# Position bias by four float32 column products instead of masks and three-piece products, in a fused attention, expert and cosine layer

## The chip, the cores and the metric

The kernel runs on one core of one Trainium2 chip. The metric is the device time of one execution in microseconds; lower is better. The engines named below are TensorE (PE, its weight loads PEld), VectorE (DVE), ScalarE (ACT), GpSimd (POOL) and the queue that issues transfers (SP).

## The reference, cut to what matters

```python
psi_rel = np.log1p(np.abs(pos[:, None] - pos[None, :]))        # S x S, S = 576
psi_i   = np.log1p(np.maximum(pos[:, None], 1.0))
x = (psi_rel / psi_i)[..., None]
h = np.maximum(x @ w1 + b1, 0.0)                               # 32 hidden values per (i, j)
bias = h @ w2                                                  # 8 heads
attn = softmax(q @ k.T / 8 + bias);  x = attn @ v              # 2 batches, 8 heads, 64 wide
out += p[:, e] * (relu(x @ w1[e]) @ w2[e])                     # 4 experts, 512 -> 1024 -> 512
h = x @ w_in;  y = (h * cos(h)) @ w_out                        # 512 -> 2048 -> 512
```

There are 1152 tokens (2 x 576).

## The kernel before, in words

Nothing in the file is written in the order in which it runs. `build` records steps (`G.step`), each with an engine, a planned duration, what it reads and writes, and a priority, and `Graph.order` then runs a list scheduler over them: whenever an engine is free it takes the ready step with the lowest priority number, with planned delays between engines. Steps with `alts` may go to a second engine after a planned wait. The instructions are issued in that order, so a changed planned duration moves instructions on every engine.

The work comes in three stretches. In the first, `bias_step` runs 36 times. Step s covers 16 query positions; 128 partitions hold 4 positions x 32 hidden values, four such groups t = 0..3 make a step. The width W of a step is 576, 512, 384 or 448 keys, the rest is mirrored from other steps. A mask per group says where the hidden value is positive: groups 0 and 1 by DVE (L508), groups 2 and 3 by ACT as a sign (L510), both written as bf16. PE multiplies the masks by two weight sets (w1*w2 and b1*w2), each cut into three bf16 pieces (L532): four column tiles of 32 columns, one for each t, which write 32 partitions of PSUM each. Two DVE operations (L540, L547) combine the two products with the table `tab2` and the row factor `nrec`. The result is stored to DRAM (`biasD`, mirrored parts to `biasR`) and later loaded again by each attention unit. Besides, `first_set` works out attention of the first 64 queries, in float32, of all heads and both batches, and `fill` runs the experts for these 128 tokens in float32, one half of an expert (512 hidden columns) at a time; NFILL of the 8 halves are done so.

In the second stretch `second_set` works out attention of the other 512 queries (float32 operands in fp32r form, each as a high and a low part, three products); its last product is at L745. Fills and expert jobs stand between its pieces on PE. In the third stretch come the experts for 2 x 512 tokens, and the cosine layer. A half of an expert is either plain (12 products of 512 columns for each 128 hidden columns and 512 tokens, L798) or blocked: `block_products` (L938) gets both 512-token blocks of the first layer with 7 products in place of 8, from sums that `block_tokens` and `block_weights` prepare. The second layer is L807 for all. NHALF halves are plain, NFILL - NHALF are blocked, the rest take in the first 128 tokens as well.

Of the kernel before, what the change touches and what calls it, by code (L numbers as in the profile page):

```python
# [33 lines left out]

class Buf:
# [18 lines left out]
class Graph:  # L54
    LAG = {"PE": 215.0, "ACT": 160.0, "DVE": 165.0, "POOL": 160.0, "DMA": 100.0}
    TO_PE = {"ACT": 250.0, "DVE": 245.0, "POOL": 175.0, "DMA": 207.0}
    SWITCH, STAY = {"columns": 93.0, "rows": 196.0, "": 196.0}, 0
# [48 lines left out]

    def order(self):
        steps = self.steps
# [32 lines left out]
        while len(out) < len(steps):  # L141
# [16 lines left out]
            for e in engs:  # L158
# [47 lines left out]
                if e == "PE" and s.mode != mode:  # L206
                    s.dur, mode = s.dur + max(0.0, self.SWITCH[s.mode] - (now - eng_free[e])), s.mode
# [6 lines left out]
                tp = s.end + s.lat + self.TO_PE.get(e, 0.0)  # L214
                heapq.heappush(events, t)
                for k in s.succ:
                    same = k.eng == s.eng == "PE"
                    k.rdy = max(k.rdy, s.end if same else tp if k.eng == "PE" else t)
                    k.nd -= 1
                    if k.nd == 0:  # L220
                        offer(k)
# [29 lines left out]
def t_col(n):  # L251

    return n / 2.4 + 3.0
# [20 lines left out]
NFILL = 7  # L274

NHALF = 2
# [3 lines left out]
FKEEP = 2  # L280
# [3 lines left out]
NWAIT = 8  # L284
SIGNED = ((36, (2, 3)),)
# [3 lines left out]
NH, NW, NB, NF, NEARLY = 8, 12, 5, 16, 14  # L289

P_GEN, P_ADD, P_SPA, P_SPD, P_E32, P_REL, P_SUB, P_NRM, P_EV, P_REV, P_TWO = 200.0, 2500.0, 150.0, 1500.0, 300.0, 300.0, 2000.0, 3000.0, 1000.0, 200.0, 0.0

O_GEN, O_SGN, O_STT, O_ADD, O_SPL, O_EVC, O_NRM = 80, 0, -150, 0, 150, -10, 0

BAHEAD, HAHEAD, FAHEAD, BACK, BACK0, G_SET, G_FILL, G_MAIN = 5, 3, 3, 4, 2, 33, 6, 1
# [30 lines left out]
def shape_constants():  # L326
# [10 lines left out]
    c = np.concatenate([tab, tab2, nrec, np.eye(128, dtype=np.float32)], axis=1)  # L337
# [3 lines left out]
NCONST = 1148 + 1136 + 36  # L341
# [3 lines left out]
def build(ctx: ExitStack, tc: tile.TileContext, consts, q, v, qd, kp, vp, w12, probs, mw1, mw2, win, wout, out):  # L345
# [10 lines left out]
    biasR = {i0: T(dr, [1032, w], F32, f"biasR{i0}") for i0, w in RW.items()}  # L356
    planes = {nm: T(dr, sh, F32, nm + "hl") for nm, sh in (
# [7 lines left out]
    w32 = T(sb, [128, 128], F32, "w32")  # L365
    wrm = w32[:, 64:128]
    wph = w32[:, 0:96].bitcast(BF16).rearrange("p (k n) -> p k n", k=3)
    hcol = w32[:, 96:98].bitcast(BF16)
    wpc = T(sb, [128, 3, 64], BF16, "wpc")
    cneg = T(sb, [128, 144], F32, "cneg")  # L370
    cpos = T(sb, [128, 144], F32, "cpos")
# [4 lines left out]
    kc = T(sm, [128, 3 + len(SIGNED)], F32, "kc")  # L376
    ca = kc[:, 3:3 + len(SIGNED)]
# [23 lines left out]
    G.add_class("B", [T(pb_, [128, 2304], BF16, f"bs{i}") for i in range(NB)])  # L401
    cst = T(pb_, [128, NCONST], F32, "cst")
    tab = cst[:, 0:1148]
    tab2 = cst[:, 1148:2284]
    nrec = cst[:, 2284:2320]
# [16 lines left out]
    def dma(nbytes, fn, **kw):  # L422
        return G.step("DMA", t_dma(nbytes), fn, lat=LAT, **kw)
# [6 lines left out]
    dma(128 * 640 * 4, lambda: nc.sync.dma_start(out=cst[:, 508:1148], in_=consts[:, 508:1148]), wr=[(cb, "r1")])  # L430
    dma(128 * 1172 * 4, lambda: nc.sync.dma_start(out=cst[:, 1148:2320], in_=consts[:, 1148:2320]), wr=[(cb, "t2")])
    dma(128 * 508 * 4, lambda: nc.sync.dma_start(out=cst[:, 0:508], in_=consts[:, 0:508]), wr=[(cb, "r0")])
    dma(18432, lambda: nc.sync.dma_start(out=prob, in_=probs.rearrange("p (t e) -> p t e", e=NE)), wr=[fix("prob")])
    dma(128 * 128 * 4, lambda: nc.sync.dma_start(out=ident, in_=consts[:, 2320:2448]), wr=[fix("ident")])
# [9 lines left out]
    for kk in range(2):  # L444
        G.step("DVE", 130, lambda kk=kk: nc.vector.tensor_scalar(
            out=w32[:, 32 * kk:32 * kk + 32], in0=wpad, scalar1=prm[:, kk:kk + 1], scalar2=(1.0, 8.0)[kk], op0=ALU.mult, op1=ALU.mult),
            rd=[fix("prm")], wr=[(fix("w32"), kk)], port=True)
    for kk in range(3):
        src = w32[:, 0:64] if kk == 0 else wrm
        G.step("DVE", 130, lambda kk=kk, src=src: nc.vector.tensor_copy(wpc[:, kk, :], src), rd=[fix("w32")], wr=[fix("w32"), fix("wpc")], port=True)  # L450
        if kk < 2:
            G.step("DVE", 130, lambda kk=kk, src=src: nc.vector.tensor_tensor(out=wrm, in0=src, in1=wpc[:, kk, :], op=ALU.subtract),
                   rd=[fix("w32")], wr=[fix("w32")], port=True)
    G.step("DVE", 180, lambda: nc.vector.tensor_scalar(out=wph, in0=wpc, scalar1=0.5, scalar2=None, op0=ALU.mult),
           rd=[fix("wpc")], wr=[fix("w32"), fix("wph")], port=True)
    G.step("DVE", 120, lambda: (nc.vector.memset(hcol[:, 0:2], 0.5), nc.vector.memset(hcol[:, 2:4], 0.0)), rd=[fix("wph")], wr=[fix("w32"), fix("hcol")])
    cp = Buf("P1")

    def half_sums():
        for j, (_, ts) in enumerate(SIGNED):  # L460
            for i in range(3):
# [29 lines left out]

    def bias_step(s, back, p2, gates=()):

        u_, mk = Buf("E"), Buf("B")
        sj, ts = signed(s)
        ka, kb = key_range(s)
        W = kb - ka
# [870 lines left out]
```

## Time and profile before

| | |
|---|---|
| median of 3 runs | 794.1 us (793.37 to 860.72) |
| the profiled execution, its own time | 796.37 us |
| its span in the trace | 794.6 us |
| PE busy | 778.1 us (98%), 5134 matmul records |
| DVE busy | 667.7 us (84%) |
| ACT busy | 446.6 us (56%) |
| POOL busy | 162.7 us (20%) |
| granted TensorE clock | 1.0 in all 40 slices of the span |

A matmul's record is longer than the time until the next one can start, so a busy share of 98% doesn't mean that PE has no time left to lose. Where a price of a matmul is needed, it is taken from long unbroken runs of one kind: their time divided by their count.

### The profile page before, as it was taken

How to read it: one execution, taken by the hardware profiler on the slowest of the kernel's cores; microseconds unless marked ns; L12 is line 12 of the kernel's file. 1: busy time of each engine (PE TensorE's matmuls, PEld its weight loads, DVE VectorE, ACT ScalarE, POOL GpSimd, SP SyncE). 2: the span in 40 equal slices, each digit the busy share in tenths (PEclk: the TensorE clock that was granted, in tenths of full speed). 3: DMA queues.
4: the chain of work that ended last, by engine and by line, in shares of the span. 5: the costliest groups of instructions: out<-in, count | busy, mean ns of one | idle time of the engine just before them, and what ended most of it. 6: DMA issues, size and time to landing. Idle time of an engine off the chain costs nothing.

```text
span 794.6 us, 14995 instructions
## 1 busy us (share of the span) xinstructions
PE 778.1 (98%) x5134; PEld 647.6 (81%) x5134; DVE 667.7 (84%) x1560; ACT 446.6 (56%) x942; POOL 162.7 (20%) x215
## 2 busy tenths in 40 slices
PE   7899999999999999999999999999999999999998
PEld 6476667887888888887888888888889889998997
DVE  8978978998999997766997979799789949959575
ACT  7677468888887533334462627263635637545352
POOL 0121077788755520234000000000000000000000
PEclk9999999999999999999999999999999999999999
DMA  6898999788865214645644346344473297547012
GB/s 194 288 289 249 297 285 307 225 280 265 267 193 186 80 54 136 206 150 185 226 146 154 124 159 201 111 139 168 145 244 108 85 339 250 174 136 262 27 40 80
DMA packets 98988, 148.08 MB, mean 186 GB/s; under 512 B 13280, under 2 KB 46688, under 8 KB 98912
## 3 DMA queue, kind: packets, MB, share of 16 engines
q1 hardware_dynamic: 98912, 147.13, 57.0%
q8 instruction: 40, 0.66, 0.4%
q14 instruction: 36, 0.29, 0.1%
HBM read 110.68 MB, written 36.41 MB: 185 GB/s over the span
## 4 chain that ended last, share of the span: by engine, by line
PE 73%; DVE 10%; DMA 8%; ACT 4%; issue 3%; SPq 1%; DVEq 0%; ACTq 0%
PE p1x L807 18%; PE p L807 12%; PE p1x L938 8%; PE p1x L798 7%; PE p L938 7%; PE p L798 4%; PE p L532 4%; PE p L745 3%; PE p L677 2%; PE p L725 2%; DMA fs<-in_mw 2%; PE p L1053 2%; DMA biasD<-es 1%; ACT es L650 1%; PE p L1061 1%
## 5 line engine op out<-in xcount | busy, mean ns | idle before, releaser
L807 PE MATMUL p1x<-wx,hs 128*128 128x512 f32 (+1 forms) x792 | 185.1, 389 | 0.5 <-DVE fs L1018 0.5
L807 PEld LDWEIGHTS p1x<-wx,hs 128*128 128x128 f32 x792 | 147.3, 188 | 31.9 <-DVE fs L1018 0.9
L807 PE MATMUL p<-wx,hs 128*128 128x512 f32 (+1 forms) x432 | 102.9, 389 | 0.2 <-DVE hs L1004 0.2
L807 PEld LDWEIGHTS p<-wx,hs 128*128 128x128 f32 x432 | 79.7, 188 | 16.6 <-DVE hs L1004 0.6
L798 PE MATMUL p1x<-xh,wx 128*128 128x512 f32 (+2 forms) x272 | 79.0, 361 | 1.3 <-DVE hs L1004 1.2
L660 POOL TENSOR_SCALAR es<-es,stats 128x576 f32<-128x576 f32 (+2 forms) x102 | 62.8, 632 | 44.6 <-DVE stats L654 17.3
L573 ACT ACTIVATE wx<-fs 128x512 fp32r<-128x512 f32 (+1 forms) x83 | 46.4, 581 | 32.3 <-DMA fs<-in_mw 20.6
L650 ACT ACTIVATE es<-es,stats 128x576 f32<-128x576 f32 x72 | 55.3, 770 | 10.6 <-DVE stats L647 4.2
L532 PE MATMUL p<-bs,wpc 128*32 128x288 bf16 (+3 forms) x576 | 51.1, 323 | 7.4 <-DVE es L547 3.6
L798 PEld LDWEIGHTS p1x<-xh,wx 128*128 128x128 f32 x272 | 50.0, 188 | 7.9 <-DVE hs L1004 2.5
L647 DVE CUSTOM_DVE_ANT_0 es<-p,es 128x576 f32<-128x576 f32 x72 | 53.0, 749 | 3.8 <-PE p L725 1.4
L574 DVE TENSOR_TENSOR wx<-fs,wx 128x512 fp32r<-128x512 f32 (+1 forms) x68 | 44.2, 674 | 9.7 <-ACT wx L573 9.7
L532 PEld LDWEIGHTS <-wpc 128*32 128x32 bf16 x576 | 30.8, 97 | 23.5 <-issue 14.2
L532 PE MATMUL p<-bs,w 128*32 128x288 bf16 (+3 forms) x576 | 49.9, 322 | 0.0
L510 ACT ACTIVATE bs<-cst,cpos 128x576 bf16<-128x576 f32 (+3 forms) x72 | 45.6, 694 | 7.2 <-PE p L532 4.7
L798 PE MATMUL p1x<-xl,wx 128*128 128x512 f32 (+2 forms) x136 | 48.9, 359 | 0.0
L938 PE MATMUL p1x<-xh,wx 128*128 128x512 f32 (+1 forms) x140 | 45.7, 368 | 0.0
L585 DVE TENSOR_TENSOR hs<-p,hs 128x512 fp32r<-128x512 f32 x61 | 41.3, 686 | 3.7 <-ACT hs L583 3.1
L573 ACT ACTIVATE fs<-fs 128x256 fp32r<-128x256 f32 x54 | 21.8, 413 | 39.7 <-DVE fs L1127 39.6
L677 PE MATMUL p<-ident,es 128*128 128x128 f32 x276 | 42.2, 280 | 0.4 <-ACT x L707 0.3
L798 PE MATMUL p<-xh,wx 128*128 128x384 f32 (+2 forms) x144 | 39.9, 341 | 0.0
L677 PEld LDWEIGHTS p<-ident,es 128*128 128x128 f32 x276 | 30.4, 140 | 10.8 <-issue 6.1
(232 smaller groups left out, 1751.2 us busy)
## 6 DMA issues: line engine op xcount, KB each, us to landing
fs<-in_mw SPq DMA_DIRECT2D x123, 256.0 KB, 4.4
wx<-winhl SPq DMA_DIRECT2D x32, 256.0 KB, 4.7
wx<-wouthl SPq DMA_DIRECT2D x32, 256.0 KB, 3.9
wouthl<-fs SPq DMA_DIRECT2D x29, 256.0 KB, 2.4
fs<-in_win SPq DMA_DIRECT2D x28, 256.0 KB, 4.2
es<-biasD SPq DMA_DIRECT2D x24, 288.0 KB, 3.9
fs<-in_wout SPq DMA_DIRECT2D x27, 256.0 KB, 3.5
winhl<-fs SPq DMA_DIRECT2D x25, 256.0 KB, 2.8
```

The source lines that it names most:

```text
L510: G.step("ACT", t_act(W, 1, 1), lambda w0=w0, u=u, t=t: nc.scalar.activation(out=mask(t), in_=tab[:, w0:w0 + W], func=AF.Sign, bias=cpos[: ...
L532: nc.tensor.matmul(out=pv(a)[32 * t:32 * t + 32], lhsT=w[:, i, 32 * kk:32 * kk + 32], rhs=mask(t, m * a, m), start=(i == 0), stop=(i == 2) ...
L573: act = ("ACT", t_act(n, 0, 1), lambda: nc.scalar.activation(out=hv(), in_=fv(), func=AF.Copy))
L574: low = lambda e: e.tensor_tensor(out=lv(), in0=fv(), in1=hv().bitcast(F32), op=ALU.subtract)
L585: G.step("DVE", t_dve(n), lambda: nc.vector.tensor_tensor(out=dst(AL), in0=src(), in1=dst(AH).bitcast(F32), op=ALU.subtract), rd=[ps_, (AH ...
L647: G.step("DVE", t_dve(S) + 10, lambda: nc.vector.tensor_tensor_reduce(out=f3(bt.tile[:, :S]), in0=sp.tile[:, :, 0:288], in1=f3(bt.tile[:, ...
L650: exp_all.append(G.step("ACT", t_act(S, 1, 1) + 104, lambda: nc.scalar.activation(out=e.tile[:, :S], in_=bt.tile[:, :S], func=AF.Exp, scal ...
L660: nrm = lambda g: g.tensor_scalar(out=dst(), in0=src(), scalar1=rs, scalar2=1.0, op0=ALU.mult, op1=ALU.mult)
L677: nc.tensor.transpose(tp.tile[:, 128 * kt:128 * kt + 128], e.tile[:, 128 * kt:128 * kt + 128], ident)
L798: nc.tensor.matmul(out=z.tile[:, 0:n], lhsT=w[dt][2][wi]()[:, 128 * ft:128 * ft + 128], rhs=x[:, dt, p0:p0 + n], start=(dt == 0 and i == 0 ...
L807: nc.tensor.matmul(out=y.tile[:, 0:m], lhsT=hx, rhs=w[ft][2][wi]()[:, c0:c0 + m], start=(ft == 0 and i == 0), stop=(ft == nf - 1 and i == 2))
L938: nc.tensor.matmul(out=z.tile[:, 0:n], lhsT=x()[:, 128 * t:128 * t + 128], rhs=y(), start=(start and d == 0 and i == 0), stop=(d == 1 and ...
```

## The change

The masks go. Each group's hidden value itself, relu(w1*psi_rel + b1*psi_i), is written in float32 (DVE by add and max, ACT by Relu; either may take it), PE multiplies it by the padded w2 in one float32 matmul per column tile, and one scaling by `nrec` (ACT, or DVE) evacuates the product. The weight pieces, the half sums and `tab2` fall away. Then: NFILL 7 to 8 and NHALF 2 to 1, so that seven halves of experts are blocked in place of five; `block_tokens` loads the whole float32 values, stored to DRAM beforehand (`x1D`, `x2D`), in place of adding up high and low parts (14 DVE operations for each of four blocks become 8); the planner's delays and durations are changed, and 17 seeded changes of priorities (`MOVES`) are made ahead of planning.

```diff
     def order(self):
+        for m in MOVES:
+            self.move(m)
...
-NFILL = 7
-NHALF = 2
+NFILL = 8
+NHALF = 1
...
-        u_, mk = Buf("E"), Buf("B")
+        u_, hid = Buf("E"), [Buf("B"), Buf("B")]
...
-                e.tensor_scalar(out=mask(t), in0=tab[:, w0:w0 + W], scalar1=cneg[:, u:u + 1], scalar2=None, op0=ALU.is_ge)
-                    out=mask(t), in_=tab[:, w0:w0 + W], func=AF.Sign, bias=cpos[:, u:u + 1]), rd=rdt + [fix("cpos")], wr=[(mk, t)], after=gate, off=O_SGN)
+            act = ("ACT", t_act(W, 1, 1), lambda w0=w0, u=u, t=t: nc.scalar.activation(
+                out=hv(t), in_=tab[:, w0:w0 + W], func=AF.Relu, bias=cpos[:, u:u + 1]))
+            dve = ("DVE", t_dve(W, 1, True), lambda w0=w0, u=u, t=t: nc.vector.tensor_scalar(
+                out=hv(t), in0=tab[:, w0:w0 + W], scalar1=cpos[:, u:u + 1], scalar2=0.0, op0=ALU.add, op1=ALU.max))
...
-            def mm(kk=kk, pv=pv):
-                for i in range(3):
-                    for a in range(npc):
-                        for t in range(4):
-                            w = wph if t in ts else wpc
-                            nc.tensor.matmul(out=pv(a)[32 * t:32 * t + 32], lhsT=w[:, i, 32 * kk:32 * kk + 32], rhs=mask(t, m * a, m),
-                                             start=(i == 0), stop=(i == 2), tile_position=(0, 32 * t))
+        def mm():
+            for a in range(npc):
+                for t in range(4):
+                    nc.tensor.matmul(out=pv(a)[32 * t:32 * t + 32], lhsT=wpad, rhs=hv(t, m * a, m), start=True, stop=True, tile_position=(0, 32 * t))
+        bias_mm[s, 0] = G.step("PE", 4 * npc * t_col(m), mm, rd=hid + [fix("prm")], wr=[pb], mode="columns")
...
-        G.step("DVE", t_dve(W, 1), lambda: nc.vector.scalar_tensor_tensor(
-            G.step("DVE", t_dve(n, 1), lambda pc=pc, uv=uv, n=n: nc.vector.scalar_tensor_tensor(
+        G.step("ACT", t_act(W, 1), lambda: nc.scalar.activation(out=uo(), in_=pi(), func=AF.Copy, scale=nrec[:, s:s + 1]),
+               rd=[pb, (cb, "r1")], wr=[(u_, 0)], off=O_STT,
+               alts=[("DVE", t_dve(W, 1), lambda: nc.vector.tensor_scalar(
...
+        x1_st[p, b] = dma(128 * Q1 * 4, lambda: nc.sync.dma_start(out=x1D[p, :, Q1 * b:Q1 * b + Q1], in_=x32.tile[:, :Q1]), rd=[x32])
...
+                dma(128 * n * 4, lambda: nc.sync.dma_start(out=b.tile[:, 0:n], in_=whole[dd, :, n * c:n * c + n]), wr=[b], after=stored(dd, c) + after)
```

On PE the first bias step reads as follows before; `bs` are the masks, `wpc` and `w_76` the bf16 pieces of the weights, `p_160` a bank pair in PSUM, and this pattern comes back for each of three pieces, for both halves of the width, and for both weight sets:

```order
L532 LDWEIGHTS wpc
L532 MATMUL p_160<-bs_147,wpc 32x288
L532 LDWEIGHTS wpc
L532 MATMUL p_160<-bs_147,wpc 32x288
L532 LDWEIGHTS w_76
L532 MATMUL p_160<-bs_147,w_76 32x288
L532 LDWEIGHTS w_76
L532 MATMUL p_160<-bs_147,w_76 32x288
```

In the same place of the changed kernel the first four rows are one whole step (two halves of the width, four tiles each) and the fifth begins the next; `bs` are now hidden values, `prm` holds the padded w2, and a row with x2 is two column tiles:

```order
L506 MATMUL p20_160<-bs0_146,prm_77 32x288 x2
L506 MATMUL p20_160<-bs4_150,prm_77 32x288 x2
L506 MATMUL p20_160<-bs0_146,prm_77 32x288 x2
L506 MATMUL p20_160<-bs4_150,prm_77 32x288 x2
L506 MATMUL p21_161<-bs1_147,prm_77 32x288 x2
```

A step of two halves has gone from 48 matmuls, piece after piece with the four tiles in turn, to 8 float32 ones, each tile complete before the next begins; the whole program has 1152 and 192.

On DVE, early in the program, masks (L508) stand before between the combinations of the two products (L540, L547) and the first softmax operations (L647, L654, L656):

```order
L508 TENSOR_SCALAR bs_148<-cst,cneg 128x512 x2
L540 SCALAR_TENSOR_TENSOR es_143<-p_153,kc,cst 128x512
L508 TENSOR_SCALAR bs_147<-cst,cneg 128x384
L647 ISA es_137,stats<-p_160,es_137 128x576
L647 ISA stats 128x1
L508 TENSOR_SCALAR bs_147<-cst,cneg 128x384
```

After the change the rows of that stretch are nearly all hidden values (L495), while on ACT (the second piece) hidden values (L493) and evacuations (L511) take turns:

```order
L495 TENSOR_SCALAR bs_146<-cst,cpos 128x512
L495 TENSOR_SCALAR bs_148<-cst,cpos 128x512
L495 TENSOR_SCALAR bs_146<-cst,cpos 128x512
L470 RECIPROCAL psum_p<-psum_p 128x9
L495 TENSOR_SCALAR bs_147<-cst,cpos 128x512
```

```order
L493 ACTIVATE bs0_146<-cst_152,cpos_78 128x576
L511 ACTIVATE es1_128<-p21_161,cst_152 128x576
L493 ACTIVATE bs1_147<-cst_152,cpos_78 128x576
L511 ACTIVATE es2_129<-p20_160,cst_152 128x576
L493 ACTIVATE bs2_148<-cst_152,cpos_78 128x512
```

In all, DVE has 90 hidden values and 13 evacuations where it had 72 masks and 80 combinations, and ACT has 54 and 23 where it had 72 signs. In the order after, 6 units of the first 64 queries have passed ACT before its last bias operation, 8 before.

On PE behind the last attention product (L745 before, L711 after; `ht` is its last operand) the order before goes on with the experts' second layer:

```order
L745 MATMUL p1x_3823<-ht_95,ks_120 128x256
L807 MATMUL p1x_3832<-wx_3041,hs_90 128x512
L807 MATMUL p1x_3832<-wx_3042,hs_90 128x512
L807 MATMUL p1x_3832<-wx_3041,hs_90 128x512
L807 MATMUL p1x_3832<-wx_3276,hs_94 128x512
```

and after the change with pieces of fills (L1022, L1014), among first-layer products (L765):

```order
L711 MATMUL p_156<-ht_94,ks_119 128x256
L1022 MATMUL p_153<-fs_99,fs_113 128x512
L1022 MATMUL p_153<-fs_105,fs_113 128x512
L1022 MATMUL p_153<-fs_103,fs_113 128x512
L765 MATMUL p_156<-xh,wx_2200 128x512
```

Parts of the last three fills (32 float32 matmuls at L1014, 12 at L1022) now stand behind the attention, where none stood before.

## Rows read from the trace of the kernel before

**Rows 1.** The page's first part: busy time and share of each engine.
```profile
PE 778.1 (98%) x5134; PEld 647.6 (81%) x5134; DVE 667.7 (84%) x1560; ACT 446.6 (56%) x942; POOL 162.7 (20%) x215
```

**Rows 2.** Busy time by stretch; the second line names the columns.
```profile
core 0: us, PE busy (x) PEld busy (x) DVE busy (x) ACT busy (x) POOL busy (x), PEclk, DMA share, GB/s
0.00:102.20 102.20, 93.51 (x1411) 66.32 (x1412) 89.52 (x216) 66.76 (x131) 12.93 (x25) 1.00 0.83 263
102.20:258.20 156.00, 153.34 (x1205) 125.30 (x1205) 140.69 (x412) 126.60 (x294) 111.88 (x153) 1.00 0.81 251
258.20:794.60 536.40, 531.25 (x2520) 455.95 (x2519) 437.51 (x934) 253.30 (x518) 37.91 (x38) 1.00 0.46 153
```

**Rows 3.** Lines L532 and L745: count, ns min/median/max, first and last start.
```profile
L532 PE MATMUL p<-bs,w x576: 286/326/441, 6.5 to 101.8; 128*32 128x288 bf16 x96, 128*32 128x448 bf16 x40, 128*32 128x512 bf16 x32, 128*32 128x384 bf16 x24
L745 PE MATMUL p1x<-ht,ks x1: 283/283/283, 257.9 to 257.9; 128*128 128x256 f32 x1
```

**Rows 4.** Bias products by shape: count, busy us, mean ns, idle before.
```profile
L532 PE MATMUL p<-bs,w 128*32 128x288 bf16 x288 | 20.1, 289 | 0.0
L532 PE MATMUL p<-bs,w 128*32 128x448 bf16 x120 | 12.4, 353 | 0.0
L532 PE MATMUL p<-bs,w 128*32 128x512 bf16 x96 | 11.6, 380 | 0.0
L532 PE MATMUL p<-bs,w 128*32 128x384 bf16 x72 | 6.9, 327 | 0.0
```

**Rows 5.** Bias matmuls and weight loads in order of time: start us, us.
```profile
71.53 0.37 PE L532 MATMUL p<-bs,wpc 128*32 128x448 bf16 x2
...
71.72 0.37 PE L532 MATMUL p<-bs,wpc 128*32 128x448 bf16 x2
...
83.30 0.10 PEld L532 LDWEIGHTS <-w 128*32 128x32 bf16 x2
...
83.42 0.29 PE L532 MATMUL p<-bs,wpc 128*32 128x288 bf16 x2
83.54 0.29 PE L532 MATMUL p<-bs,wpc 128*32 128x288 bf16 x2
```

**Rows 6.** Unbroken runs in the chain that ended last: start us, us, what.
```profile
1.05 5.06 PE p L439 x22
170.11 1.79 PE p L1053 x16
188.72 1.72 PE p L1061 x4
679.78 4.16 PE p1x L798 x24
717.75 5.44 PE p1x L807 x24
```

**Rows 7.** DVE groups of 0 to 102.2 us: busy us, mean ns, idle before.
```profile
L508 DVE TENSOR_SCALAR bs<-cst,cneg 128x576 bf16<-128x576 f32 (+3 forms) x72 | 31.7, 468 | 0.1
L547 DVE SCALAR_TENSOR_TENSOR es<-es,cst,p 128x288 f32<-128x288 f32 (+4 forms) x43 | 26.7, 630 | 0.8 <-PE p L532 0.7
L540 DVE SCALAR_TENSOR_TENSOR es<-p,kc,cst 128x576 f32<-128x576 f32 (+3 forms) x36 | 25.7, 725 | 3.7 <-PE p L532 2.4 <-DMA biasD<-es 1.1
```

**Rows 8.** ACT groups of 0 to 102.2 us, and one evacuation of later.
```profile
L510 ACT ACTIVATE bs<-cst,cpos 128x576 bf16<-128x576 f32 (+3 forms) x72 | 45.6, 694 | 7.2 <-PE p L532 4.7 <-DVE wpc L450 1.6 <-ACT bs L510 0.7
L650 ACT ACTIVATE es<-es,stats 128x576 f32<-128x576 f32 x8 | 6.2, 776 | 6.7 <-DMA biasD<-es 2.2 <-DVE stats L647 1.2 <-PE p L692 1.2
...
L589 ACT ACTIVATE es<-p 128x512 f32<-128x512 f32 (+1 forms) x9 | 4.6, 523 | 1.0 <-PE p L677 0.8
...
L583 ACT ACTIVATE hs<-p 128x512 fp32r<-128x512 f32 x61 | 35.6, 593 | 6.1 <-PE p L677 5.3
```

**Rows 9.** Whom PE waited for in 0 to 102.2 us: total, times, longest.
```profile
PE p L532 <- DVE es L547: 3.6, 3, 1.8
```

**Rows 10.** Line L473, a DVE operation that writes float32: ns min/median/max.
```profile
L473 DVE TENSOR_SCALAR cst<-cst,prm x2: 484/518/552, 4.1 to 6.8; 128x640 f32<-128x640 f32 x1, 128x508 f32<-128x508 f32 x1
```

More of the change, by code (lines that the diff above doesn't have):

```diff
@@ L105, in step, with move @@
         return s
+    def move(self, seed):
+        r = random.Random(seed)
+        lines = sorted({s.line for s in self.steps})
+        n = len(self.steps)
+        line, first, share = r.choice(lines), r.randrange(-n // 10, n), r.choice((0.01, 0.03, 0.1, 0.3, 1.0))
+        kind, by = r.random(), r.choice((-1, 1)) * r.choice((3, 10, 30, 80, 200, 500))
+        for s in self.steps[max(first, 0):max(first + int(n * share), 0)]:
+            if s.line != line:
+                continue
+            if s.lat and kind < 0.5:
+                s.lat = max(1500.0, s.lat + 5 * by)
+            elif len(s.alts) > 1 and kind < 0.5:
+                s.alts = s.alts[:1] + [(*a[:3], max(0.0, a[3] + 5 * by)) for a in s.alts[1:]]
+            else:
+                s.prio += by
     def order(self):
+        for m in MOVES:
+            self.move(m)
         steps = self.steps
@@ L422, in dma @@
     def dma(nbytes, fn, **kw):
[L423 removed]
+        return G.step("DMA", t_dma(nbytes), fn, lat=LAT if kw.get("wr") else LATS, **kw)
     def f3(t, n=2):
@@ L499, in bias_step @@
         m = W // npc
-        mask = lambda t, c0=0, n=W: mk.tile[:, 576 * t + c0:576 * t + c0 + n]
+        hv = lambda t, c0=0, n=W: hid[t // 2].tile[:, 576 * (t % 2) + c0:576 * (t % 2) + c0 + n]
         gate = list(gates) + ([bias_mm[s - back, 0]] if (s - back, 0) in bias_mm else [])
+        ts = next(x for end, x in ON_ACT if s < end)
         for t in range(4):
@@ L890, in block @@
-            two(lambda: xl[:, d, c1], t4v, lambda: xh[:, d, c1].bitcast(F32), ALU.subtract, [t4, (fix(t4n), (d, "h"))], [(fix(t4n), (d, "l"))], n,
-                after=done + last_l1)
+                return x
+            (b22, v22), (b12, v12), (b11, v11), (b21, v21) = load(d + 2, 1), load(d, 1), load(d, 0), load(d + 2, 0)
+            u = Buf("F")
+            uv = lambda: u.tile[:, 0:n]
+            x = two(uv, v22, v12, ALU.subtract, [b22, b12], [u], n)
+            keep_("T3", uv, u)
+            two(v12, v12, v11, ALU.subtract, [b12, b11], [b12], n, after=[x])
@@ new lines, in block @@
+            x = [x, keep_("T1", v12, b12)]
+            two(v22, v22, v12, ALU.subtract, [b22, b12], [b22], n, after=x)
+            keep_("T2", v22, b22)
+            two(v21, v21, v22, ALU.subtract, [b21, b22], [b21], n)
+            G.step("ACT", t_act(n, 0, 1), lambda: nc.scalar.activation(out=xh[:, d, c1], in_=v21(), func=AF.Copy),
+                   rd=[b21], wr=[(fix(t4n), (d, "h"))], after=last_l1)
+            two(lambda: xl[:, d, c1], v21, lambda: xh[:, d, c1].bitcast(F32), ALU.subtract, [b21, (fix(t4n), (d, "h"))], [(fix(t4n), (d, "l"))], n,
+                after=last_l1)
@@ L1258, in build @@
     run_ff(jobs, m2_ev1, m2_ev2, xr2)
-    tk2 = block_tokens(pcols, lambda d, x: range(3 * x + 3, 3 * x + 6), NP, [], ("x2h", "x2l"), "t4b")
+    tiles = lambda d, c: range(3 * c + 3, 3 * c + 6)
+    tk2 = block_tokens(pcols, tiles, NP, x2D, lambda d, c: [x2_st[t] for t in tiles(d, c)], [], ("x2h", "x2l"), "t4b")
     for c in range(NCONV, LATE):
```

200 lines of the change are left out of this document (64 added, 136 removed).

## The prediction

> **What bounds the kernel now.** I read the page's first part, then busy time by stretch, then in each stretch what its engines wait for. PE is busy 98% of the span and no other engine over 84% [rows 1]. But busy time of overlapping matmul records hides lost time, so I cut the span at two places that the change touches: the last bias product, whose matmul starts at 101.8 us, and the last attention product, which starts at 257.9 us [rows 3]; with the matmuls' own length the cuts are 102.2 and 258.2. The reader should see three different stretches [rows 2].
>
> In the last one (536.4 us) PE runs 2520 matmuls back to back. Runs of one kind give prices: 24 products of 512 columns take 5.44 us, 0.227 each, and 24 of 384 take 4.16, 0.173 each [rows 6]; 256 columns are 0.120 on the same line. The 2520 matmuls (1824 of 512, 588 of 384, 72 of 256, 36 transposes at the 0.11 of a float32 record of 128 columns) come to 528 us, so only 8 us are lost there, the end included. That stretch is PE's.
>
> The middle one (156.0 us) is nearly PE's: PE 153.3 busy, DVE 140.7, ACT 126.6.
>
> The first one (102.2 us) is different. DVE is busy 89.5 us of it, ACT 66.8 [rows 2], and bias products wait for DVE's combinations (the largest entry is 3.6 us in 3 waits, the longest 1.8) [rows 9]. PE's own need is smaller than its 93.5 busy us. A set of four bf16 column tiles repeats after 0.19 us at 448 columns (71.53 to 71.72) and after 0.12 at 288 (83.42 to 83.54) [rows 5], so the four run side by side. Records by shape, 288 of 288 columns in one of the two names and so on, make 24 pieces of 288, 10 of 448, 8 of 512 and 6 of 384 columns, six sets each [rows 4]: (24 x 0.122 + 10 x 0.189 + 8 x 0.215 + 6 x 0.162) x 6 = 45 us. With warming up (5.1), 32 and 4 matmuls of fills (7.2 + 3.4) and the first attention set (7.8 for scores, 9.0 for its products with v, 4.4 for transposes) PE needs 82 us of 102.2. These prices follow below.
>
> So the time is the end of the bias stretch, plus the middle one, plus PE's work behind it. I price the three.
>
> **The last stretch: +9 us.** More of the work stands here, though the program as a whole has less. Behind the last attention product the order has 1848 matmuls of 512 columns (+24, +5.4 us), 540 of 384 (-48, -8.3), 24 of 256 (-48, -5.8), and pieces of fills. A float32 matmul is two records: 11 warm-up matmuls are 22 records. Sixteen records of 128 columns take 1.79 us, 0.112 each; four of 512 take 1.72, 0.430 each [rows 6]. The 32 and 12 float32 matmuls cost 64 x 0.112 + 24 x 0.430 = 17.5. Sum +8.9, and the stretch is 545.3 us. What falls away elsewhere (24 DVE operations of `block_tokens`, six more ACT copies, the stores and loads of whole values) I cost at nothing: DVE is busy 437.5 us of 536.4 here, ACT 253.3, DMA 0.46 [rows 2], and the first product on loaded values has over 50 us of PE work between it and the last attention product. If that cover were gone, one store and one load would show, a few us each.
>
> **The middle stretch: +4.4 us.** Fills here go from 80 and 24 matmuls to 96 and 20 (+3.6, -3.4); the end of the first attention set slips in (15 matmuls at L667 +3.4, 4 at L658 of 288 columns, 0.243 a record, +1.9, 15 transposes +1.6); 12 products at L807 leave (-2.7). 156.0 + 4.4 = 160.4. Bounds: 154 if DVE (which had 90% of it) set the pace rather than PE, 164 if the other order packs worse.
>
> **The first stretch: from 102.2 to 67 us.** Here the chief gain lies.
> DVE: the 72 masks become 90 values; writing float32 costs no more than bf16, since 508 and 640 columns of float32 took 484 and 552 ns [rows 10], on the line of the masks' mean of 468 [rows 7]. 31.7 x 90/72 = 39.6, +7.9. The combinations go (25.7 + 26.7); 13 evacuations at 725 ns come (+9.3). With two attention units moved behind (-2.3), DVE falls from 89.5 to about 52.
> ACT: 54 values for 72 signs, at 694 ns, -12.5; 23 evacuations from PSUM. A plain one of 512 columns took 593 ns, the signs with their per-partition operand 694 [rows 8]: +13.6 to +16. Two exponentials (776 ns and a read of the sum) and five copies (523) have moved behind, with some small ones: -7. ACT comes to 61 to 63 us from 66.8 and is now the busiest of the two. DVE, the busiest before, was busy 0.875 of this stretch; nothing that waits on small prelude operations is left at its head, and the ready values queue up, so I take 0.93 for ACT: 62.5 / 0.93 = 67 us. Bounds: 62 (the two share perfectly) and 76 (ACT at 0.82).
> PE: bias 192 float32 matmuls, 384 records. At 2n/2.4 GHz + 5 ns, which gives the measured 0.112 and 0.430, one record is 0.245, 0.325, 0.378, 0.431 us for 288, 384, 448, 512 columns; one record per piece is 15.0 us in all. If four tiles run side by side as bf16 ones do, two such slots make a piece: 30 us for 45. With warming up 5.1 and the first set's share (12 float32 matmuls of 288 columns, 25 of 128, 25 transposes: 14), PE needs 49 of the 67: hidden behind ACT. No row shows float32 column tiles, so this is the unknown; the nearest row is the set of four tiles [rows 5], and I take it.
>
> By the Trainium skill (TensorE: Matmul & The Clock Gate, Part 3, "The mechanism") only weight loads pass matmuls that wait; matmuls start strictly in program order. The trace agrees as far as it goes: a weight load of the next set is at 83.30, its matmul at 83.42 [rows 5]. The same skill (TensorEngine Tiling (Array Packing), Key Properties) lets different tiles work in parallel. By the second the sum stands; by the first it is the first rival's 800.
>
> **Sum.** 67 + 160.4 + 545.3 = 772.7 us of span. The profiled execution had 794.6 of span in 796.37 us, 1.8 around it, and is 2.3 above the median of the runs: so 772 in the median's terms, 2.8% below 794.1. Its own range, from the bounds, is 760 to 784.
>
> **The rivals.**
> 1. *Float32 tiles that wait for themselves: no change, 800 us.* In the order each tile's two records follow each other. If the second holds back the next tile's first, slots go: first of tile 0; second of 0 with first of 1; and so on, four slots a piece and one more a step: 60 to 72 us. PE then needs 79 to 91 in the first stretch, with its losses there 95, and it bounds the stretch: 95 + 160.4 + 545.3 = 801. For it: in every set of the trace the four tiles stand next to each other, so nothing there shows a tile passing a waiting one. Against it: nothing but the side-by-side rows. Chance 0.18.
> 2. *The first stretch stays bound by transfers or ACT: about 783 us.* Bias stores (9 MB and 2 mirrored), most of the first set's keys and values and their bias loads, from the shapes some 19.5 MB, must pass; the stretch now moves 263 GB/s at a share of 0.83 [rows 2]: 74 us at that rate, 62 at a full share. At 78 us the sum is 784. Chance 0.07.
> 3. *Float32 column tiles don't share the array: slower, 855 us.* Eight slots a piece are 120 us; the first stretch becomes 150, the sum 856. It decides for slower from some 105 us of first stretch, about five slots a piece. Against it: bf16 tiles share it in every set. Chance 0.05.
>
> **Chances.** The forecast has 0.70. A measurement tells 2% from no change: faster below 778, slower above 810. The forecast ends below 778 about 8 times in 10 (0.57, as its bounds reach 784), with little from the rivals: faster 0.60. The rest of it, rival 2 and nearly all of rival 1: same 0.34. Rival 3 and the tail of 1: slower 0.06. The range 760 to 800 holds the forecast (0.68), rival 2 (0.07) and a third of rival 1.
>
> **What would show each step right or wrong.** At L506, the distance between the first records of two tiles of a set: about 5 ns for the forecast, one slot (0.245 us at 288 columns) for rival 1; and its whole time, 30, 60 to 72, or 120 us. The last start at L506: 67 us, 95 for rival 1. ACT's share of the first stretch at 0.9 or more, DVE's near 0.8. The last product at L711 near 227 us, and behind it 545 us. The prediction would be wrong if the middle stretch grows as the first shrinks (its units waiting for DVE or loads of bias), or if PE idles behind the attention for loads of `x1D`.

## The result, and the profile after

The changed kernel takes 780.4 us (median of 4 runs, 780.2 to 781.2). The ratio to the kernel before is 0.983, with a 95% interval of 0.981 to 0.985: faster by 1.7%, just inside the 2% up to which the prediction calls a result the same. One of the runs before, of 860.7 us, was a slow one, and the ratio leaves it out. 772 was predicted, with 760 to 800 as the range. The profiled execution has a span of 778.5 us. The page's busy times after, as in [rows 1]:

```profile
PE 761.0 (98%) x4310; PEld 623.0 (80%) x4310; DVE 641.6 (82%) x1521; ACT 455.7 (59%) x960; POOL 126.2 (16%) x181
```

Lines L506 (bias products) and L711 (products of attention with v), as in [rows 3]: count, ns min/median/max, first and last start. The two last starts, with the matmul's own length, give the cuts 68.7 and 237.5.

```profile
L506 PE MATMUL p<-bs,prm x384: 405/458/618, 5.6 to 68.2; 128*32 128x288 f32 x96, 128*32 128x448 f32 x40, 128*32 128x512 f32 x32, 128*32 128x384 f32 x24
...
L711 PE MATMUL p<-ht,ks x30: 279/283/284, 96.7 to 237.2; 128*128 128x256 f32 x30
```

Busy time by stretch after, as in [rows 2]:

```profile
0.00:68.70 68.70, 62.11 (x506) 29.97 (x507) 55.61 (x149) 59.78 (x117) 7.76 (x15) 1.00 0.82 269
68.70:237.50 168.80, 160.94 (x1270) 134.54 (x1270) 137.47 (x413) 131.80 (x307) 116.61 (x163) 0.98 0.85 269
237.50:778.50 541.00, 537.91 (x2536) 458.53 (x2534) 448.53 (x959) 264.07 (x538) 1.82 (x3) 1.00 0.51 168
```

So the three stretches are 68.7, 168.8 and 541.0 us, where 67, 160.4 and 545.3 were predicted and 102.2, 156.0 and 536.4 stood before. The first gave 33.5 us, the other two took 17.4 back.

A sum by matmul shows more than busy shares do. Give each matmul of the trace the time until the next can start, by the prediction's prices (n columns: n/2.4 + 13 ns; float32: two records of 2n/2.4 + 5 ns; four column tiles side by side, the second set's scores two by two), and add up. This is TensorE's *need*; the rest of a stretch is *lost*. From 300 to 550 us of the changed kernel need and time agree to 0.1 us in every 50, so the prices hold. By need and loss:

| us | need: first, middle, last | sum | lost: first, middle, last | sum |
|---|---|---|---|---|
| before | 79.9, 136.1, 527.6 | 743.6 | 22.3, 19.9, 8.8 | 51.0 |
| after | 46.9, 141.0, 536.3 | 724.2 | 21.8, 27.8, 4.7 | 54.3 |

The need fell by 19.4 us, of which 15 are the bias products and 4.3 the halves of experts. The loss grew by 3.3: 8 more in the middle stretch, 4 fewer in the last. The two together are the 16.1 us between the spans of the two profiled executions; by the medians the gain is 13.7.

**Where the middle stretch loses.** Its first 39 us against those of before, by windows (columns as in [rows 2]); the first row is the kernel before, the second the changed one:

```profile
102.20:142.00 39.80, 38.27 (x301) 29.51 (x301) 33.37 (x102) 31.51 (x72) 28.95 (x40) 1.00 0.95 300
```

```profile
68.70:108.00 39.30, 32.01 (x240) 26.09 (x240) 25.65 (x86) 26.06 (x63) 24.64 (x34) 0.91 0.85 271
```

Need there is 32.5 us before and 23.1 after: 7.3 lost against 16.2. The rest of the stretch loses 12.6 and 11.6. So the whole of the growth lies in the first 39 us behind the last bias product. What was there before and is missing after are the fills, first layer (L1053 before, L1014 after):

```profile
L1053 PE MATMUL p<-x,fs x224: 273/275/377, 72.0 to 242.3; 128*128 128x128 f32 x112
```

```profile
L1014 PE MATMUL p<-x,fs x216: 271/276/378, 106.9 to 249.7; 128*128 128x128 f32 x108
```

Before, fills began 30 us ahead of the last bias product; after, 38 us behind it: they need the result of the first 64 queries, whose last product with v now ends at 82 us, and then their weights. From 69 to 107 us TensorE has only the ends of the first attention set and the beginnings of the second, each a chain through four engines. Whom it waits for there (total, times, longest):

```profile
PE p L643 <- POOL es L626: 1.8, 3, 1.1
PE p L691 <- DVE stats L613: 1.8, 2, 1.5
PE p L667 <- ACT es L555: 1.4, 2, 0.8
```

All waits of TensorE there come to 7.1 us. The clock of 0.91 in the row above can account for some 3.5 more (9% of 39.3); how the rest of the 16.2 divides the profile doesn't show.

The other kernels of the experiments below fit: the three with masks have 64 records of first-layer fills ahead of their last bias product and lose 7 to 8 us in the 39 behind it; every kernel with the new step and no added work has none there, starts its fills 31 to 38 us behind, and loses 13 to 16, whatever its order. That the missing fills are the cause is argued from this, as no run could move fills back. The fillers of the last experiment put 3.2 us of other work into the gap, and the middle stretch was 1 us longer for it (168.4 us, for 167.4 at the same clock without them), so some two thirds of it hid there in this one pair of executions.

### The profile page after: what moved, and what is told of

Same layout as the page of the kernel before. It is cut to its first block, busy times and chain, and to the rows that moved or that the text cites. A ratio compares the mean times of both kernels' runs of the same rounds, so it can differ in the third digit from the quotient of the medians.

```text
span 778.5 us, 13310 instructions
## 1 busy us (share of the span) xinstructions
PE 761.0 (98%) x4310; PEld 623.0 (80%) x4310; DVE 641.6 (82%) x1521; ACT 455.7 (59%) x960; POOL 126.2 (16%) x181
## 4 chain that ended last, share of the span: by engine, by line
PE 90%; ACT 3%; DVE 2%; DMA 2%; issue 1%; SPq 1%; POOL 0%; DVEq 0%; ACTq 0%; POOLq 0%
PE p L774 30%; PE p L895 16%; PE p1x L895 7%; PE p L765 6%; PE p1x L774 5%; PE p L711 4%; PE p L643 4%; PE p L691 3%; PE p L1014 3%; PE p L1022 3%; PE p1x L765 3%; PE p L506 1%; PE p L667 1%; ACT bs L493 1%; DMA biasR<-fs 1%
## 5 line engine op out<-in xcount | busy, mean ns | idle before, releaser
L774 PE MATMUL p<-wx,hs 128*128 128x512 f32 (+1 forms) x1020 | 234.4, 389 | 0.0
L774 PEld LDWEIGHTS p<-wx,hs 128*128 128x128 f32 x1020 | 190.5, 188 | 39.0
L895 PE MATMUL p<-xh,wx 128*128 128x512 f32 (+1 forms) x220 | 72.5, 377 | 0.0
L616 ACT ACTIVATE es<-es,stats 128x576 f32<-128x576 f32 x72 | 55.4, 771 | 13.3 <-DVE stats L613 9.5
L895 PE MATMUL p<-tx,wx 128*128 128x512 f32 (+1 forms) x240 | 57.9, 377 | 0.0
L540 DVE TENSOR_TENSOR wx<-fs,wx 128x512 fp32r<-128x512 f32 (+1 forms) x86 | 54.0, 641 | 3.0 <-POOL wx L538 1.6
L765 PE MATMUL p<-xh,wx 128*128 128x384 f32 (+1 forms) x176 | 50.7, 357 | 0.0
L895 PEld LDWEIGHTS p<-tx,wx 128*128 128x128 f32 x240 | 44.3, 188 | 7.4
L895 PEld LDWEIGHTS p<-xh,wx 128*128 128x128 f32 x220 | 41.1, 188 | 6.6
L774 PE MATMUL p1x<-wx,hs 128*128 128x512 f32 (+1 forms) x192 | 45.9, 388 | 0.0
L506 PE MATMUL p<-bs,prm 128*32 128x288 f32 (+3 forms) x384 | 40.8, 483 | 2.9 <-DVE es L513 2.1
L895 PE MATMUL p<-xl,wx 128*128 128x512 f32 (+1 forms) x110 | 41.4, 377 | 0.0
L774 PEld LDWEIGHTS p1x<-wx,hs 128*128 128x128 f32 x192 | 35.0, 188 | 7.2 <-issue 0.5
L495 DVE TENSOR_SCALAR bs<-cst,cpos 128x576 f32<-128x576 f32 (+3 forms) x90 | 38.1, 476 | 2.1 <-PE p L506 1.8
```

Of the source, the lines that this page charges most:

```text
L495: dve = ("DVE", t_dve(W, 1, True), lambda w0=w0, u=u, t=t: nc.vector.tensor_scalar(out=hv(t), in0=tab[:, w0:w0 + W], scalar1=cpos[:, u:u + ...
L506: nc.tensor.matmul(out=pv(a)[32 * t:32 * t + 32], lhsT=wpad, rhs=hv(t, m * a, m), start=True, stop=True, tile_position=(0, 32 * t))
L540: low = lambda e: e.tensor_tensor(out=lv(), in0=fv(), in1=hv().bitcast(F32), op=ALU.subtract)
L616: exp_all.append(G.step("ACT", t_act(S, 1, 1) + 124, lambda: nc.scalar.activation(out=e.tile[:, :S], in_=bt.tile[:, :S], func=AF.Exp, scal ...
L765: nc.tensor.matmul(out=z.tile[:, 0:n], lhsT=w[dt][2][wi]()[:, 128 * ft:128 * ft + 128], rhs=x[:, dt, p0:p0 + n], start=(dt == 0 and i == 0 ...
L774: nc.tensor.matmul(out=y.tile[:, 0:m], lhsT=hx, rhs=w[ft][2][wi]()[:, c0:c0 + m], start=(ft == 0 and i == 0), stop=(ft == nf - 1 and i == 2))
```

## The experiments

Every ratio is to runs of the kernel before on the same chip. Stretches and lost time are from each kernel's own profiled execution, cut and summed as above.

**What bounds the first stretch: four probes.** Each adds work for one engine to the changed kernel. All instructions otherwise keep their order.

```diff
-            for a in range(npc):
+            for a in [x for x in range(npc) for _ in range(1 + s % 2)]:
```

> The changed kernel with the bias products of every second step issued twice (the second pass overwrites the same result), in the same order of all else. That adds 15.1 us of TensorE time to the first stretch, by the slots of 0.245 to 0.431 us. My theory: in the first stretch ScalarE and VectorE set the pace and TensorE needs 47 of 68.7 us, so the extra work is hidden: last bias product at 68 to 72 us, the whole time +0 to +4 us. Rival A, TensorE bounds the kernel throughout and the change gained because TensorE's need fell by 19.4 us: +13 to +15 us. Rival B, transfers bound the stretch from 8 to 104 us: +0 to +3 us.

```diff
-            act = (... lambda ...: nc.scalar.activation(out=hv(t), ...))
+            act = (... lambda ...: [nc.scalar.activation(out=hv(t), ...) for _ in range(1 + (s % 3 == 0))])
```

> The changed kernel with ScalarE's hidden values of every third bias step computed twice (21 more operations of 0.6 to 0.78 us, some 14.6 us), in the same order of all else. My theory (ScalarE is the busiest in the first stretch, 59.8 of 68.7 us): last bias product at 79 to 83 us, the whole time +9 to +14 us. Rival A (TensorE bounds): +0 to +4. Rival B (transfers bound 8 to 104 us; what the bias loses is waited for by transfers anyway): the last bias product later by up to 10 us, but the whole time +0 to +6.

The same edit on VectorE's `dve`:

> The changed kernel with VectorE's hidden values of every third bias step computed twice (27 more operations of some 0.42 us, 11.4 us), in the same order of all else. My theory: VectorE is busy 55.6 of 68.7 us and comes to 67, so it takes over as the bound: +4 to +8 us on the first stretch and on the whole time. Rival A: +0 to +3. Rival B: +0 to +4.

```diff
-dma_start(out=biasD[128 * s:128 * s + 128, ka:ke], in_=u_.tile[:, :ke - ka])
+[dma_start(out=x[128 * s:128 * s + 128, ka:ke], in_=u_.tile[:, :ke - ka]) for x in ([biasD, biasX] if s % 2 else [biasD])]
```

> The changed kernel with the stored bias of every second step stored a second time, to a DRAM table that nothing reads (18 more stores, 4.5 MB, 14 to 17 us at 263 to 330 GB/s), in the same order of all else. My theory (a DMA share of 0.82 in the first stretch leaves 12 us free, and the stretch behind it waits for TensorE's own work): +0 to +5 us. Rival A: +0 to +3. Rival B, transfers bound the stretch from 8 to 104 us, so that each megabyte there costs its 3 us: +12 to +17 us on the whole time, and the last attention product later by the same.

Measured: 791.5, 792.8, 792.0 and 787.1 us, ratios 0.994, 0.996, 0.993 and 0.988. First stretch of the four by windows, one kernel a fence, products, ScalarE, VectorE and stores in turn:

```profile
0.00:80.60 80.60, 76.20 (x698) 37.53 (x698) 56.37 (x149) 61.28 (x116) 7.48 (x15) 1.00 0.73 238
```

```profile
0.00:82.00 82.00, 68.04 (x506) 30.72 (x506) 56.43 (x149) 73.57 (x137) 7.29 (x15) 0.98 0.69 224
```

```profile
0.00:80.30 80.30, 65.70 (x506) 30.68 (x507) 67.93 (x176) 61.61 (x116) 7.78 (x15) 0.98 0.70 230
```

```profile
0.00:74.10 74.10, 62.63 (x506) 29.95 (x506) 55.84 (x149) 60.12 (x116) 8.41 (x15) 1.00 0.88 291
```

The reader is to compare the added work with the stretch's growth over 68.7. TensorE: 15.1 us added, +11.9. ScalarE: 13.8 added (73.57 less 59.78), +13.3. VectorE: 12.3 added (67.93 less 55.61), +11.6. Stores: 4.5 MB added, +5.4. Middle and last stretch stay as they are (167.3 to 168.7 and 541.0 to 541.3). On the spans that is +11.0, +11.8, +10.6 and +5.4. By the ratios, which leave out what one chip differs from another, it is 8.6, 10.2, 8.3 and 4.5 us, each to some 3. In the second and third fence the clock is 0.98, in the changed kernel 1.00, so up to 2 us of these two growths can be the clock. My theory holds for ScalarE and nearly for the stores; for TensorE (+0 to +4 expected) and VectorE (+4 to +8) it falls, and rivals A and B fall with ScalarE's row. None of the three engines hides another: although TensorE needs 47 us of 68.7, four fifths of what it gets more show, and of the other two nearly all, less what the clock took. The chain of waits says the same from the other side, since it runs through ScalarE early and through TensorE late (start us, us, what; the changed kernel):

```profile
8.40 0.66 ACT es L511
9.05 0.66 ACT bs L493
9.72 0.63 ACT es L511
10.35 0.66 ACT bs L493
...
45.18 0.96 PE p L506 x8
46.14 1.50 PE p L667 x10
47.64 1.18 PE p L506 x16
```

The delay grows over all 36 steps, not in one place (doubled products, ends of steps counted from 0: +2.4 us at step 6, +5.4 at 13, +9.5 at 27, +12.0 at 35, the last). In the code, values wait for the product four steps back and for one of six buffers (two a step), so that a delay of one engine comes round to the others; that this ring is the cause was not tried by itself. Transfers are not the bound: 4.5 MB cost 5.4 us, not 14. That the middle stretch is up to 1.5 us shorter than in the changed kernel is no taking up of the delay; the last experiment shows it to be the clock.

**What each part is worth alone.** The bias step alone on the kernel before (values, product and evacuation as in the diff of the change, `NB` 6):

> The kernel before with the bias step alone exchanged (hidden values, one float32 product per column tile, one evacuation; six buffers for values, without tab2 and the weight pieces); halves of experts, block_tokens, the planner's numbers as before, and no MOVES. My theory: the first stretch falls to 67 to 73 us, and since TensorE's need falls by 15 us in all, the whole time falls by 10 to 20 us, as the rest of the 30 us comes back as work moved behind. Rival C (the order is what counts: without seeds that mend it, the hole behind the first stretch eats the gain): the first stretch as short, but the whole time only -5 to +5 us.

The halves alone:

```diff
-NFILL = 7
+NFILL = 8
-NHALF = 2
+NHALF = 1
```

> The kernel before with NFILL 8 and NHALF 1 alone (seven blocked halves). My theory, by the prediction's own terms without the bias (-48 products of 384 columns, -48 of 256, 24 of 512 more, one more fill): TensorE's need falls by 4 to 5 us and the time by 0 to 5 us; the first stretch stays at 102. Rival D (blocked halves free VectorE or spare waits in the last stretch, which is where the changed kernel lost 4 us less than before): -5 to -10 us.

The whole change without seeds:

```diff
-MOVES = (
-    5776518, 7495620, 1919961, 1016330, 2269784, 8008244, 9818753, 8415745, 9562368, 4819295,
-    6215312, 5267250, 9199552, 96413, 7479963, 9482709, 4094016,
-)
+MOVES = ()
```

> The changed kernel with an empty MOVES. All work is the same, only the order on the engines differs. My theory (the gain is work taken out, and seeds only trim): +0 to +6 us against the changed kernel, most of it in the stretch from the last bias product to the last attention product. Rival C (the order is what counts): +10 to +20 us, which takes back the whole gain over the kernel before.

Then two kernels with seeds found for them. The first is the kernel before with the halves, the planner's numbers and 30 seeds; the second has the new bias step besides, but the old `block_tokens`:

> The kernel before (masks, bf16 pieces, block_tokens as before) with NFILL 8 and NHALF 1, the planner's delays and durations of the changed kernel, and 30 seeds of MOVES found for it in the same way (changes of priority that shorten the planned time). It asks what an order mended by seeds gives without the new bias step. My theory now: time is TensorE's need (739 us here, 724 in the changed kernel) plus what is lost between; the kernel before lost 51, halves alone 58, and seeds can take some 10 of that: 783 to 790 us where before has 795 to 798. Rival H (seeds only mend the hole that the short first stretch makes): no gain, 793 to 798. Rival I (the whole gain of the change is the order): as fast as the changed kernel, 777 to 782.

> The new bias step, NFILL 8 and NHALF 1, the planner's numbers of the changed kernel and 31 seeds of its own, but block_tokens as before (sums of high and low parts, no x1D and x2D) and the other constants of the kernel before. TensorE's need is that of the changed kernel, 724 us. My theory (block_tokens costs nothing either way, and one set of seeds is as good as another): the time of the changed kernel within 5 us, a ratio of 0.977 to 0.989 to the kernel before. Rival J (the last stretch lost only 4.8 us after the change because block_tokens gave VectorE room): 4 to 6 us slower, all of it in the stretch behind the last attention product. Rival K (seeds are worth less on the chip than in the plan, and those of the changed kernel were chosen by its time on the chip): 8 us slower or more.

Last, the changed kernel with 29 other seeds, found by the planned time alone:

```diff
-    5776518, 7495620, 1919961, 1016330, 2269784, 8008244, 9818753, 8415745, 9562368, 4819295,
+    2983418, 966493, 3757104,
...
```

> The changed kernel, word for word, with 29 other seeds in MOVES, found from an empty list by the planned time alone; the plan comes out as long as that of the changed kernel. The work is the same (TensorE's need 724 us), the order is another. Theory L (what the seeds give in the plan they give on the chip): 778 to 783 us, a ratio of 0.979 to 0.986 to the kernel before. Rival K (the seeds of the changed kernel are better on the chip than plans of equal length are on the average, so part of the gain is that choice): 784 to 790, a ratio of 0.986 to 0.992.

| kernel | ratio (95%) | first, middle, last | need | lost |
|---|---|---|---|---|
| bias alone | 0.997 (0.995 to 1.000) | 72.8, 160.4, 557.1 | 728.5 | 61.8 |
| halves alone | 0.999 (0.997 to 1.001) | 103.6, 161.1, 532.7 | 739.3 | 58.1 |
| all, without seeds | 1.003 (1.000 to 1.006) | 75.1, 170.8, 553.0 | 724.2 | 74.7 |
| masks, halves, seeds | 0.996 (0.994 to 0.997) | 102.3, 157.5, 531.0 | 739.3 | 51.5 |
| new bias, old tokens, seeds | 0.989 (0.986 to 0.992) | 76.2, 158.9, 550.2 | 724.2 | 61.1 |
| all, other seeds | 0.981 (0.977 to 0.985) | 73.6, 156.1, 547.7 | 724.2 | 53.2 |
| the change | 0.983 (0.981 to 0.985) | 68.7, 168.8, 541.0 | 724.2 | 54.3 |

Several things follow. The bias step alone shortens the first stretch by 29 us and the whole by 2, so rival C holds there: fills that ran beside the bias now run behind the attention, the last stretch is 20.7 us longer, and the loss grows by 11, 8 of it in the middle stretch. My theory of 10 to 20 us falls. The halves alone took 4.3 us from the need, as expected, and 0.1% from the time (0 to 5 us expected; rival D falls), since the loss grew by 7. The whole change without its seeds is no faster than the kernel before; the seeds are worth 16 us by the ratios and 20 us of loss in the profiled executions, so rival C holds again, and my 0 to 6 was wrong. Up to 6 of these 20 can be the clock, whose mean was 0.989 without seeds and 0.996 with them (1.1% of 799 us less 0.4% of 778). They aren't all of it: the same means on the kernel with masks give 0.4% (793.0 us: rival I falls, my 783 to 790 as well, and rival H's no gain nearly holds). And other seeds give as much as those of the change (theory L), with stretches that differ by 5 to 13 us each: need is a property of the work, the stretches are one of the order.

Where the seeds' gain lies is not where I looked for it. Of the 20 us, 3 are each in the first two stretches and 14.7 in the last. The kernel without seeds from 400 to 600 us, where the blocked halves and the first of the cosine layer run, by windows and by TensorE's waits:

```profile
400.00:600.00 200.00, 191.84 (x840) 155.65 (x839) 170.94 (x387) 93.39 (x198) 0.00 (x0) 0.99 0.53 170
```

```profile
PE p1x L892 <- ACT fs L899: 4.4, 3, 2.0
PE p L892 <- ACT fs L899: 2.0, 1, 2.0
PE p1x L892 <- DVE fs L902: 1.2, 2, 0.7
PE p L892 <- DVE fs L902: 0.5, 1, 0.5
```

The changed kernel there:

```profile
400.00:600.00 200.00, 200.00 (x921) 168.47 (x920) 186.19 (x419) 104.34 (x220) 0.00 (x0) 1.00 0.61 198
```

Products of the blocks (L892) wait for the copies (L899) and sums (L902) of the products before them, 8.1 us of the 12.7 lost there; the clock of 0.99 can account for 2 more. With seeds TensorE has no wait in these 200 us, and VectorE is busy 186 of them. With the old `block_tokens` the time is 0.7% longer, 5.3 us, so my 5 us just fail to hold. It loses 6.9 us in the last stretch against 4.7 to 4.9 with the new one (rival J, in half its size); the other 5 us of that kernel's loss lie in the first two stretches, and since constants beside `block_tokens` differ too, what they are due to stays open.

**The order of the column tiles.**

```diff
-            for a in range(npc):
-                for t in range(4):
+            for t in range(4):
+                for a in range(npc):
```

> The changed kernel with the two loops around the bias products exchanged: in the 12 steps of 576 keys each column tile gets its two 288-column products one behind the other, in place of all four tiles in turn; the order is the same in all else. My theory (a tile that is busy lets the products of other tiles pass only as far as the next one or two matmuls): the eight products of a step take 5 slots of 0.245 us or more in place of 4, so L506 takes 3 to 6 us more over the 12 steps, and the time is +2 to +5 us. Rival E (every tile has a queue of its own): the same 4 slots, +0 us. Rival F (strictly in order, as the prediction's first rival): 7 to 8 slots, +9 to +12 us in the first stretch.

780.4 us, ratio 0.980 (0.978 to 0.982), stretches 68.9, 167.4, 541.0. The last two steps of 576 keys, 32 records in all, in order of time (start us, us), in the changed kernel and in this one:

```profile
66.46 2.15 PE L506 MATMUL p<-bs,prm 128*32 128x288 f32 x32
```

```profile
66.69 2.19 PE L506 MATMUL p<-bs,prm 128*32 128x288 f32 x32
```

Rival E holds: the order costs nothing that shows in the first stretch.

**The half clock behind the bias.** From 76 to 80 us the granted clock of the changed kernel is 0.58 (between the levels of 1.2 and 2.4 GHz), behind TensorE's waits of 72 to 76. The probe fills these waits:

```diff
         def trn():
+            for _ in range({6: 5, 7: 2, 8: 2}.get(c, 0)):
+                nc.tensor.matmul(out=tp.tile[:, 0:128], lhsT=ident, rhs=ident, start=True, stop=True)
...
         def av():
+            for _ in range({6: 3, 7: 2}.get(4 * b + p, 0)):
+                nc.tensor.matmul(out=bank.tile[:, 128:256], lhsT=ident, rhs=ident, start=True, stop=True)
```

> The changed kernel with 14 products of the identity by itself (128 columns, float32, 0.225 us each, 3.2 us in all; what they write is overwritten at once) where TensorE waits behind the last bias product: ahead of the transposes of units 6, 7 and 8 (5, 2, 2) and of two products with v (3, 2). The order is the same in all else. It asks what the granted clock of 0.58 from 76 to 80 us costs, which follows TensorE's wait from 73 to 76. Theory M (the half clock there is on the path: ten products at L667 took 2.66 us for 1.50, four transposes 1.09 for 0.66): the clock of 76 to 80 comes back to 1.0 and the stretch from the last bias product to the last attention product is 1 to 2 us shorter. Rival N (other waits end last there, so the clock costs nothing): the same to 0.5 us; if the fillers stand in the way, up to 2 us longer.

780.3 us, ratio 0.981 (0.978 to 0.984), stretches 69.3, 168.4, 541.1. Windows of 72 to 80 us, of the changed kernel and of the probe:

```profile
72.00:76.00 4.00, 2.11 (x11) 1.31 (x11) 2.23 (x8) 1.75 (x6) 0.74 (x1) 0.99 0.93 303
76.00:80.00 4.00, 3.63 (x15) 2.86 (x14) 0.49 (x2) 0.59 (x2) 2.79 (x3) 0.58 0.65 191
```

```profile
72.00:76.00 4.00, 3.73 (x24) 2.72 (x22) 1.85 (x8) 2.02 (x6) 0.74 (x1) 1.00 0.91 280
76.00:80.00 4.00, 3.43 (x25) 2.92 (x25) 1.15 (x5) 0.75 (x3) 2.79 (x3) 1.00 0.76 235
```

The clock is at 1.00, and yet the second scores of the next attention set start where they did. Before that is read as a clock that costs nothing, a third kernel belongs beside the two: the one with the loops around the bias products exchanged, whose order behind the last bias product is that of the changed kernel, without fillers. Its clock did not fall there:

```profile
76.00:80.00 4.00, 3.24 (x23) 2.73 (x23) 0.76 (x5) 1.87 (x5) 3.24 (x4) 1.00 0.76 241
```

In order of time, ten products with v, the first score and the second scores of the next set, in the changed kernel, the probe (its L671 and L695 are L667 and L691 of the others) and the kernel with exchanged loops:

```profile
75.84 2.66 PE L667 MATMUL p<-es,es 128*128 128x128 f32 x10 [0.79 <-ACT es L555]
...
81.37 0.39 PE L691 MATMUL p<-ks,ks 64*128 64x288 f32 x1
...
84.60 1.05 PE L691 MATMUL p<-ks,ks 64*128 64x288 f32 x12 [1.53 <-DVE stats L613]
```

```profile
76.92 1.47 PE L671 MATMUL p<-es,es 128*128 128x128 f32 x10
...
81.57 0.39 PE L695 MATMUL p<-ks,ks 64*128 64x288 f32 x1
...
84.56 1.06 PE L695 MATMUL p<-ks,ks 64*128 64x288 f32 x12 [1.53 <-DVE stats L613]
```

```profile
76.12 1.54 PE L667 MATMUL p<-es,es 128*128 128x128 f32 x10 [0.79 <-ACT es L555]
...
80.10 0.40 PE L691 MATMUL p<-ks,ks 64*128 64x288 f32 x1
...
83.33 1.07 PE L691 MATMUL p<-ks,ks 64*128 64x288 f32 x12 [1.53 <-DVE stats L613]
```

From the ten products to the first score it is 5.53 us in the changed kernel, 4.65 in the probe and 3.98 at the full clock without fillers. The four probes of the first stretch have the full clock there too, and 3.97 or 3.98 us. So the fillers stood in the way of the steps behind them, and the probe alone can't price the clock; nor does it show that the fillers kept the clock up, which was up in five runs without them. The wait of 1.53 us for VectorE doesn't hide the clock's price either: VectorE there works on the first scores, which come later by as much.

What the full clock saves is kept to the end of the stretch, which takes 167.4 us with exchanged loops (167.3 to 167.7 in three of the four probes, 168.7 in that of the stores) for 168.8 in the changed kernel. The runs agree: with exchanged loops two took 779.5 and 779.7 us at a mean clock of 0.998, two 781.1 and 781.3 at 0.996; the changed kernel's four all had 0.996. Theory M holds in size, some 1.4 us, though not by the probe made for it; rival N holds for the probe's time alone. The waits of 1.1 and 0.8 us ahead of the ten products are the same in the changed kernel and in the one with exchanged loops, so why the clock fell in one and not in the other stays open. A second low stretch (0.78 and 0.80 from 84 to 92 us in the changed kernel) is in the probe as well (0.79 and 0.78), and was not tried.

## Why the prediction came out as it did

- **The total** was 1.1% too low. The stretches missed by +1.7, +8.4 and -4.3 us; the sum of 772.7 us of span became 778.5. The chance of 0.60 for faster by over 2% went to a result that is faster by 1.7%. That the total came this close is in part luck, since the last stretch's miss makes up for half of the middle one's.
- **First stretch, 67 us: right in size, its reason in part wrong.** VectorE's values took 38.1 us (39.6 predicted), its evacuations 9.0 (9.3); the stretch has 55.6 us of VectorE and 59.8 of ScalarE (52 and 61 to 63). ScalarE's share is 0.87, not 0.93; it had less work and a lower share than predicted, and the two misses offset each other, which is luck. But the step "PE needs 49 of the 67: hidden behind ACT" fell: what TensorE needs more shows by four fifths. So slower column tiles would have cost from the first microsecond, not from behind 18 us of cover.
- **Float32 tiles side by side: right.** Two slots a piece: 32 records of 288 columns make four pieces, 8 slots of 0.245 and the last one's own rest, in 2.15 us. The rival of tiles that wait for themselves asks for 16 slots or more, 3.9 us, and tiles one by one for 32. By the Trainium skill (TensorE: Matmul & The Clock Gate, Part 3, "The mechanism") matmuls start strictly in program order; here the products of one tile don't wait for the second pass of another's, in either order of the loops, and the measurement decides.
- **Middle stretch: the step that failed.** Its work was priced well (+4.9 us of need, +4.4 predicted), but the term kept the 20 us that the stretch before lost, where 27.8 were lost. Some 1.4 of the 8 us more are the half clock behind the bias; for the rest the likely reading is cover. The fills had covered the begin of the second attention set; the order showed that they had left the bias stretch, and I priced that as work, not as cover. The bound of 164 "if the other order packs worse" was set without a row.
- **Last stretch.** Need +8.7, +8.9 predicted. The 8 us lost before were carried over as well, and became 4.7. "Costed at nothing" holds for the whole values' stores and loads: the profile lists no wait of TensorE's matmuls behind the last attention product.
- **What no step held.** The order after was read for what it moves. That 17 changes of priority decide 16 to 20 us, more than the whole gain of 14, stood in no term and no rival.

## What to carry over

Where one engine has nearly all the work, split time into its need and what is lost, for the whole program: shortening a stretch that other work fills gives only the need that goes away, and the work that had filled it must find cover elsewhere. Where engines hand work round through few buffers, an engine's idle share may be no cover: add a known amount of work to each engine in turn and see how much of it shows. And a change to a scheduled kernel is the work and the order together; measure it once without the tuned order before crediting the work. Before a probe that found nothing is read as no cost, see whether the probe itself stood in the way, and whether other runs of the same order already hold the comparison.

## What the runs showed of the hardware

Float32 matmuls on four column tiles of 32 columns cost two slots of 2n/2.4 GHz + 5 ns for all four, and the order of issue between the tiles makes hardly a difference (2.15 and 2.19 us for 32 records of 288 columns, tiles in turn or each tile twice). Behind equal waits the granted clock fell to 0.58 over 4 us in one profiled execution and stayed at 1.00 in five others of the same order; ten products took 2.66 us for 1.54, and what followed came some 1.4 us later, up to the end of the stretch. With work put into the waits the clock was 1.00 as well, and that work took back about half of the gain.
